# Converting the last pieces of w_in later in the expert loop, and matmuls on a constant ahead of its products

## The chip, the cores and the metric

The kernel runs on one core of a Trainium2 chip. The metric is device microseconds of one execution of the whole program, median of several runs. Engines are named as the profile names them: PE (matmul) with PEld (its weight loads), DVE (VectorE), ACT (ScalarE), POOL (GpSimd) and SP (SyncE, which only issues DMAs here; SPq is its DMA queue). Each engine works through its own list of instructions in order.

## The reference

Three stages follow each other: an attention, a mixture of experts and a two-layer network. Only the middle one is touched by the change, with a piece of the third one's weights.

```python
# moe: x (1792, 768), phi (768, 32), w1 (8, 768, 1024), w2 (8, 1024, 768)
logits = x @ phi
d = softmax(logits, over tokens);  slot_input = d.T @ x        # 32 slots, 4 of each expert
for e in range(8):
    h = maximum(slot_input[e] @ w1[e], 0)
    slot_out[e] = h @ w2[e]
c = softmax(logits, over slots);   x = c @ slot_out
# moe2: w_in (768, 2048) and w_out (2048, 768) as float64, alpha (2048)
h = x @ w_in
g = maximum(h, 0) + alpha * minimum(h, 0)
out = g @ w_out
```

`softmax` stands for the reference's lines of max, exp, sum and division.

## The kernel before, in words

The attention takes the first 300 us or so, in an order that a table of numbers sets. It is the same in both kernels. Then comes the loop over the eight experts (L1325 to L1382), whose order is that of the code, and then the products of the last stage (L1528 to L1530).

**Weights.** w1 and w2 come in 32 units of 128 x 3072 float32 (1536 KB), four of an expert: two halves of w1, two of w2. Below they are numbered 0 to 31. Eleven buffers in five rings hold them; `fetch` (L465) issues the next unit on SP as soon as its buffer is free, which is when PE has used the unit eleven places earlier. From expert 4 on the order on SP is units 23 to 25, then two transfers of w_out, called `rawo` (L1281), then units 26 to 31. The first `rawo` takes the buffer of unit 22 and the second that of unit 23, so they wait for both halves of expert 5's w2 to be used. SP is a queue in order: units 26 to 31 stand behind them.

**One expert.** PE multiplies the slots with w1 (L1339, 24 matmuls in the trace). ACT copies the two halves out of PSUM as `h_sb` (L1350). PE transposes them (L1353, 8). DVE sums each half into `hT` (L1355) and clips it (L1361). PE multiplies hT with w2 (L1370, 16 matmuls for each of two units u).

**Beside it.** `narrow_in(n)` turns piece n of w_in (128 x 768) from the high words of float64 into float32: an Abs on ACT (L540) and five operations on DVE (L541, L543, L545, L548, L551). Pieces 8 to 15 are done here, by the table NARROW two each in experts 0 to 3, after the expert's sums and ahead of its w2 products. Its temporaries share two buffers, so that the Abs of a piece starts when L548 of the piece before it is done. `turn_c(b)`, in experts 2 to 5 for batches 0 to 3, makes the dispatch weights' copies: two casts on DVE (L1262), two subtractions on POOL (L1263), four transposes on PE (L1267), one copy on ACT (L1270, cT). `turn_alpha` in expert 3 turns alpha on PE (L1252) and copies it on DVE (L1253, L1254). `go_early` in expert 6 issues the conversion of the first four blocks of w_out (L498 on ACT, L500 to L510 on DVE, the cast whi L1301 on ACT, the difference wlo L1303 on DVE). Since ACT works in order, h_sb of expert 7 stands behind all of it, and the first wlo overwrites the buffer of unit 27, the second half of expert 6's w2.

Of the kernel before, what the change touches and what calls it, by code (L numbers as in the profile page):

```python
# [12 lines left out]
F16 = mybir.dt.float16  # L13
# [340 lines left out]
def fused_attention_softmoe_mlp(  # L354
# [15 lines left out]
    nc = tc.nc  # L370
    B, H, S, D = q.shape
    NT, DM = out.shape
    E, _, FE = w1.shape
# [3 lines left out]
    P = 128  # L377
# [43 lines left out]
    def pst():  # L421
        return ps.tile([P, 512], F32, tag="t", name="pst", bufs=PST)
# [13 lines left out]
    ident = const.tile([P, P], F32, name="ident")  # L436
# [52 lines left out]
    def prefetch(n):  # L489
        while len(loaded) < min(n, len(items)):  # L490
            for _ in fetch():
                pass
# [43 lines left out]
    def narrow_in(n):  # L536
        g, i = divmod(n, 4)
        w = win[g][:, i * DM : (i + 1) * DM]
        t = hp.tile([P, DM], F32, tag="wf", name="wf", bufs=2)
        nc.scalar.activation(t, w, AF.Abs)  # L540
        nc.vector.tensor_scalar_max(t, t, F64_TINY)  # L541
        b = hp.tile([P, DM], U32, tag="wf", name="wb", bufs=2)
        nc.vector.tensor_copy(b, low[:, (n - N0) * DM : (n - N0 + 1) * DM])  # L543
        t, w = t.bitcast(U32), w.bitcast(U32)
        nc.vector.tensor_scalar(  # L545
            out=t, in0=t, scalar1=3, scalar2=0x3FFFFFFF, op0=ALU.logical_shift_left, op1=ALU.bitwise_and
        )
        nc.vector.scalar_tensor_tensor(  # L548
            out=t, in0=b, scalar=5, in1=t, op0=ALU.logical_shift_right, op1=ALU.bitwise_or
        )  # L550
        nc.vector.scalar_tensor_tensor(  # L551
            out=w, in0=w, scalar=0xC0000000, in1=t, op0=ALU.bitwise_and, op1=ALU.bitwise_or
        )
# [524 lines left out]
    with tc.manual_schedule():  # L1078
# [110 lines left out]
        for o, sp, queue in (("bg0", "bgs", bg), ("pf0", "pfs", pf), ("cv0", "cvs", cv)):  # L1189
            t = T[o]  # L1190
# [30 lines left out]
    for t in range(KD):  # L1221
# [4 lines left out]
            start=True,  # L1226
            stop=True,
# [11 lines left out]
    def psa():  # L1239
        return ps.tile([P, 512], F32, tag="a", name="psa", bufs=6)  # L1240
# [8 lines left out]
    def turn_alpha():  # L1249
        pt = pst()  # L1250
        for t in range(2):
            nc.tensor.transpose(pt[:, t * 8 : t * 8 + 8], alpha_n[:, t::2], ident[: KF // 2, : KF // 2])  # L1252
        nc.vector.tensor_copy(alpha_t, pt[:, :KF].rearrange("p (t n) -> p n t", t=2))  # L1253
        nc.vector.tensor_scalar_mul(nalpha, alpha_t, -1.0)  # L1254
# [3 lines left out]
    def turn_c(b):  # L1258
        c = cN[:, b]
        cs = hp.tile([P, 4, 2, 2, NS], F32, tag="h_sb", name="cs")  # L1260
        for r in range(2):
            nc.vector.tensor_copy(cs[:, :, r, 0, :].bitcast(F32R), c)  # L1262
            nc.gpsimd.tensor_tensor(out=cs[:, :, r, 1, :], in0=c, in1=cs[:, :, r, 0, :], op=ALU.subtract)  # L1263
        pc = pst()
        for j in range(4):
            n = P if j < 3 else D
            nc.tensor.transpose(  # L1267
                pc[:, j * P : j * P + n], cs[:n, j].rearrange("p a b s -> p (a b s)"), ident[:n, :n]
            )
        nc.scalar.copy(  # L1270
            cT4[:, b * S : (b + 1) * S].rearrange("k (p c) -> k c p", c=NC),
            pc[:, :S].rearrange("k (c p) -> k c p", c=NC),
        )
# [5 lines left out]
    def fetch_out(n):  # L1279
        rawo[n] = raw = rings[1 - n % NW // (NW - NWI)][1].tile([P, UNIT], F32, tag="w", name="rawo").bitcast(U32)  # L1280
        nc.sync.dma_start(raw, w_out[2 * n * P : 2 * (n + 1) * P, :].bitcast(U32).rearrange("(p t) f -> p (t f)", p=P))  # L1281
# [33 lines left out]
    def go_early():  # L1315
        for f in EARLY_STEPS:
            next(early[f], None)

    order = ExitStack()
    order.enter_context(tc.manual_schedule())  # L1320
    pS = [psa() for _ in range(2)]
    NARROW = ((8, 9), (10, 11), (12, 13), (14, 15), (), (), (), ())
    for e in range(E):
        n = min(NRING + 4 * e, len(items))
        if len(loaded) <= T["RAWPOS"] < n or (e == E - 1 and not rawo):  # L1325
            prefetch(T["RAWPOS"])
            for i in range(NEARLY // 2):
                fetch_out(i)
        prefetch(n)
        if e == 1:  # L1330
            nc.sync.dma_start(alpha_n, alpha.rearrange("(n f) -> n f", n=KF // 2))
        ph = [psa() for _ in range(2)]
        seen = set()
        todo = [(0, 0, 0), (0, 1, 1), (0, 2, 2), (1, 0, 3), (1, 1, 0), (1, 2, 1)]
        todo += [(0, 3, 3), (0, 4, 0), (0, 5, 1), (1, 3, 2), (1, 4, 3), (1, 5, 0)]
        last = {(hf, g): t for hf, t, g in todo}
        for hf, t, g in todo:
            wu = loaded[0, e, t // 3].rearrange("p (t f) -> p t f", t=3)
            nc.tensor.matmul(  # L1339
                ph[hf][32 * g : 32 * g + 32, :],  # L1340
                slT[:, t, :],
                wu[:, t % 3, hf * 512 : (hf + 1) * 512],
                start=(hf, g) not in seen,
                stop=last[hf, g] == t,
                tile_position=(0, 32 * g),
            )
            seen.add((hf, g))
        for hf in range(2):
            h_sb = hp.tile([P, 512], F32, tag="h_sb", name="h_sb")
            nc.scalar.copy(h_sb, ph[hf])  # L1350
            pt = pst()
            for t in range(4):
                nc.tensor.transpose(pt[:, t * P : (t + 1) * P], h_sb[:, t::4], ident)  # L1353
            dst = hT[:, e, hf * 4 : hf * 4 + 4, SPE * e : SPE * e + SPE]
            nc.vector.tensor_reduce(  # L1355
                out=dst,
                in_=pt.rearrange("p (f g s) -> p f s g", f=4, g=4)[:, :, SPE * e : SPE * e + SPE, :],
                axis=AX.X,
                op=ALU.add,
            )  # L1360
            nc.vector.tensor_scalar_max(dst, dst, 0.0)  # L1361
        if e == E - 2:
            go_early()
        for n in NARROW[e]:
            narrow_in(n)
        for u in range(2):
            wu = loaded[1, e, u].rearrange("p (t f) -> p t f", t=4)
            for hf in range(2):
                for g in range(4):
                    nc.tensor.matmul(  # L1370
                        pS[hf][32 * g : 32 * g + 32, :HD],
                        hT[:, e, 4 * u + g, :],
                        wu[:, g, hf * HD : (hf + 1) * HD],
                        start=(e == 0 and u == 0),
                        stop=(e == E - 1 and u == 1),
                        tile_position=(0, 32 * g),
                    )

        if e == 3:
            turn_alpha()  # L1380
        if 2 <= e < 2 + B:
            turn_c(e - 2)  # L1382

    while len(rings) > 3:
        rings.pop()[0].close()
# [12 lines left out]
    for h in range(2):  # L1398
        pt = pst()
# [233 lines left out]
```

## Time and profile before

| what | us |
|---|---|
| median of 3 runs | 690.39 |
| lowest, highest run | 684.28, 691.68 |
| the profiled execution | 685.3 |
| its span, first to last instruction | 683.3 |

The profile is that of the one execution of 685.3 us. Its times count from the first instruction. A row of the timeline gives start, duration, engine, source line, operation, written and read tile, the shape, how many instructions are merged, and in brackets how long the engine sat idle before it and what released it.

### The profile page before, as it was taken

How to read it: one execution, taken by the hardware profiler on the slowest of the kernel's cores; microseconds unless marked ns; L12 is line 12 of the kernel's file. 1: busy time of each engine (PE TensorE's matmuls, PEld its weight loads, DVE VectorE, ACT ScalarE, POOL GpSimd, SP SyncE). 2: the span in 40 equal slices, each digit the busy share in tenths (PEclk: the TensorE clock that was granted, in tenths of full speed). 3: DMA queues.
4: the chain of work that ended last, by engine and by line, in shares of the span. 5: the costliest groups of instructions: out<-in, count | busy, mean ns of one | idle time of the engine just before them, and what ended most of it. 6: DMA issues, size and time to landing. Idle time of an engine off the chain costs nothing.

```text
span 683.3 us, 14166 instructions
## 1 busy us (share of the span) xinstructions
PE 616.2 (90%) x5670; PEld 475.9 (70%) x5670; DVE 464.9 (68%) x921; ACT 372.4 (54%) x717; POOL 191.6 (28%) x203
## 2 busy tenths in 40 slices
PE   0799998989999999998868668999999999999997
PEld 0367665666667777764323214888899999999997
DVE  5788999998789877735941444999964545454540
ACT  3799998889999998742321223776521111111110
POOL 6976666557657764111001000000000000000000
PEclk9999999999999999999988969999999999999999
DMA  4575677364456325499999799130020101010101
GB/s 138 133 239 165 188 211 204 110 189 126 131 143 200 99 76 171 123 350 391 425 424 395 283 423 400 67 120 0 1 93 1 47 1 47 1 47 0 47 1 46
DMA packets 36240, 106.89 MB, mean 156 GB/s; under 512 B 5448, under 2 KB 22352, under 8 KB 31824
## 3 DMA queue, kind: packets, MB, share of 16 engines
q1 hardware_dynamic: 36176, 106.01, 44.7%
q8 instruction: 44, 0.72, 0.5%
q14 instruction: 20, 0.16, 0.1%
HBM read 92.18 MB, written 5.51 MB: 143 GB/s over the span
## 4 chain that ended last, share of the span: by engine, by line
PE 63%; ACT 14%; DMA 9%; DVE 8%; POOL 4%; issue 2%; SPq 1%; ACTq 0%; POOLq 0%; DVEq 0%
PE psa L1530 12%; PE psa L1529 12%; PE psa L1528 11%; PE psn L818 5%; DMA unit<-in_moe_w_dram 4%; PE psv L878 4%; PE psv L868 3%; PE psa L1339 3%; ACT e L834 3%; PE psr L800 2%; DMA q<-q 2%; ACT psn L839 2%; POOL nf L717 2%; PE psa L1370 2%; ACT sp L723 1%
## 5 line engine op out<-in xcount | busy, mean ns | idle before, releaser
L1528 PE MATMUL psa<-whi,gh 128*128 128x384 f32 (+1 forms) x448 | 152.0, 339 | 0.0
L1529 PE MATMUL psa<-wlo,gh 128*128 128x384 f32 (+1 forms) x448 | 151.1, 337 | 0.0
L1530 PE MATMUL psa<-whi,gl 128*128 128x384 f32 (+1 forms) x448 | 150.8, 337 | 0.0
L809 DVE TENSOR_REDUCE m<-psr 128x1 f16<-128x448 f32 x168 | 97.7, 615 | 4.8 <-PE psr L800 4.6
L1497 ACT CAST gh<-t 128x512 fp32r<-128x512 f32 x40 | 24.9, 621 | 123.0 <-DVE t L1494 122.5
L1529 PEld LDWEIGHTS psa<-wlo,gh 128*128 128x128 f32 x448 | 84.2, 188 | 2.7
L1528 PEld LDWEIGHTS psa<-whi,gh 128*128 128x128 f32 x448 | 84.2, 188 | 2.7
L1530 PEld LDWEIGHTS psa<-whi,gl 128*128 128x128 f32 x448 | 84.1, 188 | 2.8
L878 PE MATMUL psv<-vH,e 128*128 128x65 f16 (+1 forms) x1152 | 84.2, 194 | 0.0
L878 PEld LDWEIGHTS <-e 128*128 128x128 f16 (+1 forms) x1728 | 79.3, 106 | 0.0
L1491 DVE TENSOR_SCALAR t<-pst,alpha_t 128x256 f32<-128x256 f32 x80 | 34.9, 476 | 62.9 <-PE pst L1485 62.9
L868 PEld LDWEIGHTS psv<-vR,e 128*128 128x128 f32 (+1 forms) x384 | 58.9, 176 | 20.0 <-issue 10.8
L878 PE MATMUL psv<-vL,e 128*128 128x64 f16 (+1 forms) x576 | 72.5, 193 | 0.0
L850 POOL TENSOR_TENSOR e<-ef,e 128x448 f16<-128x448 f32 x48 | 52.0, 1083 | 72.2 <-ACT ef L839 52.7
L868 PE MATMUL psv<-vR,e 128*128 128x65 f32 (+1 forms) x384 | 69.8, 263 | 0.2 <-PE psn L818 0.2
L834 ACT ACTIVATE e<-psn 128x448 f16<-128x448 f32 x120 | 65.2, 544 | 7.5 <-PE psn L818 6.2
L818 PE MATMUL psn<-q,k 128*128 128x448 f16 (+1 forms) x192 | 61.4, 361 | 7.3 <-DMA q<-q 2.0
L818 PE MATMUL psn<-qB,kB 67*128 67x448 f16 (+1 forms) x192 | 61.0, 357 | 1.6 <-DMA qB<-mr 1.4
L800 PE MATMUL psr<-k,q 128*128 128x448 f16 (+1 forms) x192 | 57.2, 374 | 3.5 <-ACT k L752 2.8
L850 DVE TENSOR_TENSOR e<-psn,e 128x448 f16<-128x448 f32 x72 | 44.4, 617 | 21.4 <-ACT psn L839 21.2
L730 POOL TENSOR_TENSOR sp<-nf,sp 128x448 f16<-128x448 f32 x48 | 49.8, 1047 | 12.2 <-ACT sp L723 11.8
L745 PE MATMUL pst<-ident,sp 128*128 128x128 f16 x336 | 27.7, 230 | 17.4 <-POOL sp L730 17.4
(178 smaller groups left out, 1091.2 us busy)
## 6 DMA issues: line engine op xcount, KB each, us to landing
unit<-in_moe_w_dram SPq DMA_DIRECT2D x26, 1536.0 KB, 12.2
unit<-in_moe_w_in_dram SPq DMA_DIRECT2D x24, 512.0 KB, 6.8
rawo<-in_moe_w_out_dram SPq DMA_DIRECT2D x8, 1536.0 KB, 13.2
unit<-in_moe_w_dram SPq DMA_DIRECT2D x36, 256.0 KB, 4.9
qk<-in_q_dram SPq DMA_DIRECT2D x12, 448.0 KB, 3.8
qk<-in_k_dram SPq DMA_DIRECT2D x12, 448.0 KB, 5.4
out_dram<-osb SPq DMA_DIRECT2D x14, 384.0 KB, 2.3
vR<-in_v_dram SPq DMA_DIRECT2D x24, 128.0 KB, 3.8
```

Of the source, the lines that this page charges most:

```text
L730: eng.tensor_tensor(out=d["sp"][:, a, :, D:], in0=d["nf"][:, a], in1=d["sp"][:, a, :, 0:D], op=ALU.subtract)
L800: nc.tensor.matmul(pn[o0:o1, :S], d["q"][:, c0 : c0 + o1 - o0], d["k"][:, h * S : (h + 1) * S], start=True, stop=True)
L809: nc.vector.tensor_reduce(out=d["m"][:, c : c + 1], in_=d.pop(("pn", c))[:, :S], axis=AX.X, op=ALU.max)
L818: nc.tensor.matmul(pe[o0:o1, :S], lhs[:, c0 : c0 + o1 - o0], rhs[:, h * S : (h + 1) * S], start=st_, stop=not st_,)
L834: nc.scalar.activation(e2[:, 0], pe[:, :S], AF.Exp, scale=0.125)
L850: eng.tensor_tensor(out=e2[:, 1], in0=ef, in1=e2[:, 0], op=ALU.subtract)
L868: nc.tensor.matmul(pv[o0:o1, slot, :], d["e", c][:, qs], d["vv"][:, h, sl * D : 4 * D + 1], start=(j == 0), stop=False,)
L878: nc.tensor.matmul(pv[o0:o1, slot, 0:wd], d["e", c][:, w // 2, qs], (vl if w == 1 else vh)[:, 4 * h + sl, 0:wd], start=(j == 0 and w == 0) ...
L1491: nc.vector.tensor_scalar(out=t0[:, cs], in0=ph[:, cs], scalar1=0.0, scalar2=alpha_t[:, f // 2, i : i + 1], op0=ALU.min, op1=ALU.mult)
L1528: nc.tensor.matmul(a, gh[f][:, ms], hi[:, hs], start=(f == 0 and not (packed and m % 2 == 1 and hf == 0)), stop=False)
L1529: nc.tensor.matmul(a, gh[f][:, ms], lo[:, hs], start=False, stop=False)
L1530: nc.tensor.matmul(a, gl[f][:, ms], hi[:, hs], start=False, stop=(f == KF - 1 and not (packed and m % 2 == 0 and hf == 1)))
```

## The change

The eight pieces 8 to 15 move from experts 0 to 3 to experts 3 (two), 4 (three) and 5 (three), and within the expert from ahead of its w2 products to the end, behind `turn_alpha` and `turn_c`. A new function `keep_on` writes eight matmuls of 128 x 256 float16 on the identity into a PSUM buffer that is free at that point. It is called from expert 3 on: ahead of each half of the w1 products, and, up to expert 6, ahead of each half of the w2 products. The first PSUM tile of the transposes is allocated at the start of the expert, since keep_on writes there.

```diff
+    def keep_on(e, junk):
+
+        if e >= 3:
+            i16 = ident.bitcast(F16)
+            for _ in range(8):
+                nc.tensor.matmul(junk[:, : 2 * P], i16[:, :P], i16, start=True, stop=True)
+
-    NARROW = ((8, 9), (10, 11), (12, 13), (14, 15), (), (), (), ())
+    NARROW = ((), (), (), (8, 9), (10, 11, 12), (13, 14, 15), (), ())
...
+        pts = [pst(), None]
...
-        for hf, t, g in todo:
+        for i, (hf, t, g) in enumerate(todo):
+            if i % 6 == 0:
+                keep_on(e, pts[0])
...
-            pt = pst()
+            pt = pts[hf] = pts[hf] or pst()
...
-        for n in NARROW[e]:
-            narrow_in(n)
         for u in range(2):
+            if e < E - 1:
+                keep_on(e, ph[0])
...
         if 2 <= e < 2 + B:
             turn_c(e - 2)
+        for n in NARROW[e]:
+            narrow_in(n)
```

On ACT, the list of the experts from the third on stands like this before (h_sb: the expert's two copies; wf<-win: the Abs of w_in's pieces; cT: the dispatch weights; wf<-rawo and whi: go_early):

```order
L1350 COPY h_sb<-psa 128x512 x2
L540 ACTIVATE wf<-win_4271 128x768 x2
L1270 CAST cT_5847<-pst 128x7x64
L1350 COPY h_sb<-psa 128x512 x2
L540 ACTIVATE wf<-win_4271 128x768 x2
L1270 CAST cT_5847<-pst 128x7x64
```

and like this in the changed kernel, for experts 3 to 6:

```order
L1270 CAST cT_5847<-pst 128x7x64
L540 ACTIVATE wf<-win_2854 128x768 x2
L1360 COPY h_sb<-psa 128x512 x2
L1270 CAST cT_5847<-pst 128x7x64
L540 ACTIVATE wf<-win_2854 128x768 x2
L540 ACTIVATE wf<-win_4271 128x768
L1360 COPY h_sb<-psa 128x512 x2
L1270 CAST cT_5847<-pst 128x7x64
L540 ACTIVATE wf<-win_4271 128x768 x3
L1360 COPY h_sb<-psa 128x512 x2
```

The pieces stood ahead of the expert's cT; they now stand behind it, and ahead of the next expert's h_sb.

On DVE, expert 3 before, from its sums to its dispatch casts (the five rows from L541 on are one piece; a second piece stands where the line of dots is):

```order
L1361 TENSOR_SCALAR hT<-hT 128x4x4
L541 TENSOR_SCALAR wf<-wf 128x768
L543 CAST wb<-low 128x768
L545 TENSOR_SCALAR wf<-wf 128x768
L548 SCALAR_TENSOR_TENSOR wf<-wb,wf 128x768
L551 SCALAR_TENSOR_TENSOR win_4271<-win_4271,wf 128x768
...
L1253 COPY alpha_t<-pst 128x16
L1254 TENSOR_SCALAR nalpha<-alpha_t 128x16
L1262 CAST cs<-cN 128x4x32 x2
```

and expert 5 in the changed kernel, from its dispatch casts to expert 6's first sum (two more pieces at the dots):

```order
L1371 TENSOR_SCALAR hT<-hT 128x4x4
L1262 CAST cs<-cN 128x4x32 x2
L541 TENSOR_SCALAR wf<-wf 128x768
L543 CAST wb<-low 128x768
L545 TENSOR_SCALAR wf<-wf 128x768
L548 SCALAR_TENSOR_TENSOR wf<-wb,wf 128x768
L551 SCALAR_TENSOR_TENSOR win_4271<-win_4271,wf 128x768
...
L1365 TENSOR_REDUCE hT<-pst 128x4x4
```

The casts moved ahead of the pieces, and the pieces now stand between one expert's casts and the next expert's sums.

## Rows read from the trace of the kernel before

**Rows 1.** The page's slices: DMA's busy share in tenths, 17.1 us each.

```profile
DMA  4575677364456325499999799130020101010101
```

**Rows 2.** Windows: us, busy time of PE, PEld, DVE, ACT, POOL; clock, DMA, GB/s.

```profile
340.00:350.00 10.00, 5.71 (x26) 1.85 (x27) 3.26 (x7) 0.97 (x1) 0.86 (x2) 0.67 1.00 421
360.00:370.00 10.00, 8.26 (x36) 3.07 (x36) 1.10 (x7) 2.14 (x3) 0.86 (x2) 0.66 1.01 426
...
374.00:375.00 1.00, 1.00 (x16) 0.35 (x11) 0.00 (x0) 0.58 (x1) 0.00 (x0) 1.00 0.54 213
381.00:382.00 1.00, 1.00 (x12) 0.53 (x12) 0.00 (x0) 0.00 (x0) 0.00 (x0) 1.00 1.03 184
```

**Rows 3.** Timeline of SP's queue, issue of the first two rawo.

```profile
380.07 1.62 SPq L1281 DMA_DIRECT2D rawo<-in_moe_w_out_dram  x2
```

**Rows 4.** Waits of SP's queue, 280 to 425 us: total, times, longest.

```profile
SPq L1281 <- PE psa L1370: 15.4, 2, 14.5
```

**Rows 5.** Timeline, expert 3's stall: alpha and dispatch weights behind the pieces.

```profile
355.57 0.40 PE L1252 MATMUL pst<-ident,alpha_n 8*128 8x8 f32 x2
360.09 0.17 DVE L1253 COPY alpha_t<-pst 128x16 f32<-128x16 f32 x1
361.69 1.20 PE L1267 MATMUL pst<-ident,cs 128*128 128x128 f32 x4 [5.72 <-POOL cs L1263]
```

**Rows 6.** Timeline, the end of the experts: go_early, experts 6 and 7.

```profile
387.55 0.56 DVE L500 TENSOR_SCALAR wf<-wf 128x768 f32<-128x768 f32 x1
...
394.07 2.79 PE L1370 MATMUL psa<-unit,hT 128*32 128x384 f32 x16 [7.06 <-DMA unit<-in_moe_w_dram]
...
400.67 0.96 DVE L1303 TENSOR_TENSOR wlo<-wf,whi 128x768 fp32r<-128x768 f32 x1 [6.93 <-PE psa L1370]
...
411.50 1.07 ACT L1350 COPY h_sb<-psa 128x512 f32<-128x512 f32 x2
...
412.13 1.98 PE L1353 MATMUL pst<-ident,h_sb 128*128 128x128 f32 x8 [4.24 <-ACT h_sb L1350]
```

**Rows 7.** Timeline, one expert's steps at the full clock (experts 2, 4, 5).

```profile
335.73 2.79 PE L1370 MATMUL psa<-unit,hT 128*32 128x384 f32 x32
...
370.09 2.79 PE L1370 MATMUL psa<-unit,hT 128*32 128x384 f32 x32
...
372.81 0.75 PE L1267 MATMUL pst<-ident,cs 128*128 128x128 f32 x4
...
373.49 3.62 PE L1339 MATMUL psa<-unit,slT 128*32 128x512 f32 x24
373.59 0.99 ACT L1270 CAST cT<-pst 128x448 fp32r<-128x448 f32 x1 [4.24 <-PE pst L1267]
...
377.04 1.55 PE L1353 MATMUL pst<-ident,h_sb 128*128 128x128 f32 x8
...
378.51 2.79 PE L1370 MATMUL psa<-unit,hT 128*32 128x384 f32 x32
```

**Rows 8.** Timeline, two pieces of w_in in expert 0, then expert 1's sums.

```profile
320.84 0.55 DVE L541 TENSOR_SCALAR wf<-wf 128x768 f32<-128x768 f32 x1
...
323.36 0.85 ACT L540 ACTIVATE wf<-win 128x768 f32<-128x768 f32 x1 [2.96 <-DVE wf L548]
...
324.24 0.56 DVE L541 TENSOR_SCALAR wf<-wf 128x768 f32<-128x768 f32 x1
...
327.64 0.21 DVE L1355 TENSOR_REDUCE hT<-pst 128x16 f32<-128x64 f32 x1
...
328.12 2.79 PE L1370 MATMUL psa<-unit,hT 128*32 128x384 f32 x32
...
328.45 0.55 DVE L541 TENSOR_SCALAR wf<-wf 128x768 f32<-128x768 f32 x1
```

**Rows 9.** Timeline, attention: float16 matmuls of 448 columns, each with a weight load.

```profile
271.16 0.36 PE L818 MATMUL psn<-q,k 128*128 128x448 f16 x1
...
271.35 0.35 PE L818 MATMUL psn<-qB,kB 67*128 67x448 f16 x1
```

## The prediction, made before the changed kernel ran

> **What bounds the kernel now.** I read the slices first, then windows, then SP's queue and the chain through the experts. In the slices DMA is at nine tenths from the end of the attention to the end of the experts, except in one slice of 7 [rows 1]. Windows of 1 us place that dip: traffic halves in the one that begins at 374 and is only just back in the one that begins at 381, so the stream stands still for some 6.5 us [rows 2]. SP's queue says why: the first rawo is issued at 380.07 [rows 3], and its kind waited 14.5 us for the w2 products of expert 5 [rows 4]. Everything behind it on SP, units 26 to 31, waits as well.
>
> PE is late there because it stalled. In expert 3 the turn of alpha is done on PE at 355.97, but DVE copies it only at 360.09, behind two pieces of w_in, and PE sat idle 5.72 us until the dispatch weights were there [rows 5]. The windows of 340 and 360 show the granted clock at a mean of 0.67 and 0.66, where the others next to them are at 1.0: after each of two such stalls PE ran at 1.2 GHz for a while [rows 2].
>
> The loop's end hangs on a second chain. DVE begins go_early at 387.55, does two blocks, and then waits 6.93 us for expert 6's w2 products, which wait for their unit; wlo starts at 400.67, and h_sb of expert 7, behind it on ACT, at 411.50 [rows 6]. What comes later is not changed, so **I forecast the shift of that wlo**.
>
> **The change, part by part.** *Taken away:* the pieces ahead of expert 2's and expert 3's dispatch casts, so two stalls of about 5.7 us and the slow matmuls behind them. Experts 0 to 2 themselves don't start earlier: PE was not held there by more than 0.2 us, so I keep expert 2's w2 products at 335.73 [rows 7].
>
> *Added: keep_on.* One batch is eight matmuls of 256 columns. The nearest row is a float16 matmul of 448 columns with its own weight load, 0.19 us from start to start [rows 9]; 256/448 of it is 0.109, so a batch takes 0.87 us at 2.4 GHz, if loads stay covered as there. Bounds: 0 would need PE to be waiting anyway, which is so for some of the batches; 1.74 if PE is at 1.2 GHz. I take 0.87. A rule of the Trainium skill speaks against the cheap batch: TensorE: Matmul & The Clock Gate, section "LDWEIGHTS (loading the stationary operand)", prices a load at its columns over 1.2 GHz, 107 ns for 128; were it not covered, a batch would be 1.73 us by an estimate from that page and my sum below 5.2 us higher. The row speaks for a covered load.
>
> *Moved: eight pieces.* A piece after another takes 3.40 us on DVE (320.84 to 324.24), two take 6.80 until the next sum, and 0.88 passes from the start of an Abs to DVE's first operation [rows 8]. The pieces now stand behind the expert's cT on ACT and ahead of the next expert's sums on DVE. So each of experts 3 to 5 becomes a ring: w2 products, turn on PE, cT, Abs, the pieces, next sums, next w2 products. I walk it with times of before; S is the start of w2 products.
>
> - Expert 3: from 335.73, 2.72 to the turn (370.09 to 372.81), 0.68 to the w1 products, two batches and 3.55 to the transposes (373.49 to 377.04), 1.55 for these [rows 7], one batch: S3 = 346.84. POOL's part of the dispatch copies is hidden behind the w2 products, as in expert 4.
> - Then 2.72 and a batch to alpha, 0.40 there, 1.60 from DVE's copy of alpha to PE's turn (360.09 to 361.69) [rows 5]: 352.43. Then 0.78 to cT (372.81 to 373.59) and 0.99 for it [rows 7], 0.88 and 6.80 for two pieces: the sums of expert 4 at 361.88. From sums to products 0.48 (327.64 to 328.12) [rows 8]: S4 = 362.36.
> - Expert 4: 2.72 + 0.87 + 0.78 + 0.99 + 0.88 + 3 x 3.40 + 0.48 = 16.92. S5 = 379.28, against 378.51 before [rows 7]. **The long ring gives back all that the stalls were worth.**
> - Expert 5 the same: S6 = 396.20, sums at 395.72.
>
> Transfers don't hold these: unit 23 lands two units ahead of the dip, about 367. The first rawo is issued 0.77 later, and so the dip stays, and unit 27 comes some 0.8 later.
>
> go_early begins 0.81 after expert 6's sums (327.64 to 328.45) [rows 8], at 396.53, 9 us later than before. Its first two blocks take 6.19 of DVE (400.67 less 387.55 less the 6.93 idle) [rows 6]: 402.72. The wait of 6.93 is nearly used up: the products that free the buffer, with unit 27 at about 398.5, are done near 401. So wlo starts at **402.72 instead of 400.67, 2.05 us later**, and h_sb of expert 7, the A stage and all products with it. The batches of experts 6 and 7 lie in DMA waits and cost nothing; if they did not, two of them behind unit 27 would be 1.7.
>
> Against the profiled execution's 685.3 us that is 687.35. It lies 5.1 below the median of 690.39, whose three runs span 684.28 to 691.68; the same 2.05 on the median gives **692.4**. About 1%, 6.9 us, is what a measurement here can tell from no change.
>
> **Rivals.**
>
> *The clock falls in the new gaps: slower.* In expert 5 of the new order w1's products end near 372.0, and h_sb stands on ACT behind the third piece's Abs, done at 375.4; transposes can start at 376.1. PE idles 4.1 us there, and about as long in expert 6; no batch stands in that gap. Before, 4.24 us of idle left the transposes of expert 7 at the lower level, 1.98 against 1.55 us, and sixteen w2 products at that level took 2.79 us [rows 6], as many as 32 at the higher [rows 7]. If expert 5 falls as well, its products and batches lose up to 2.4 (1.39 on the first sixteen and about 1.0 of what follows until the clock is back); if expert 7 stays low through its w2 products, 2.3 more (5.58 against 3.3). With 2.05 that is 6.8, or 697.2, and batches of 1.25 with loads partly uncovered make it 699.4 (six lie on the ring up to S6). It decides once the clock falls in expert 5. Against it: that gap is the shortest of those that I know to have cost the clock. Chance 0.21.
>
> *PE sets expert 5, not DVE: faster.* Without the stalls PE's own path needs 2.72 + 0.87 + 0.68 + 0.87 + 0.87 + 3.55 + 1.55 + 0.87 = 11.98 an expert, and alpha's detour puts S4 at 360.8 and S5 at 372.8. Then the first rawo goes out at 374.4, as the stream runs dry: the dip closes, worth some 6.4, which makes 684.0. The Trainium skill's page on TensorE, section "HAM oscillation", would argue this way: waits between bursts of matmuls cost the clock again each time, and a kernel that stays busy gets that time back. The windows agree that the clock was lost twice [rows 2]. But DVE's list has three pieces between the sums of experts 4 and 5, and 3 x 3.40 can't shrink by 6 us. Chance 0.09.
>
> *The two chains meet: no change.* If cT and Abs overlap and batches are hidden more than I charge, S5 comes at 378 or earlier, wlo waits for unit 27 as before, and the time is 689 to 691. Chance 0.20. That leaves 0.50 for the forecast.
>
> **Range and chances.** The forecast with its bounds runs from 690 to 695. To hold 8 in 10 I add most of the slow rival and part of the fast one, and the spread of runs of one kernel: 684.5 to 698. Faster by over 1% (under 683.5) needs the fast rival whole: 0.07. Slower by over 1% (over 697.3) needs the clock and dear batches together: 0.14. Within 1%: 0.79.
>
> **What would show it.** Right: in the changed trace no stall ahead of the turns of experts 3 and 4; clock at 1.0 from 340 to 370; pieces 10 to 12 back to back right ahead of expert 5's sums at about 379; the first rawo near 381 with the dip still there; DVE's idle ahead of the first wlo under 2 us, and wlo near 403. Wrong: expert 5's w2 products before 375 or after 383, a batch over 1.2 us, the stream without a dip, or a shift in the attention.

## The result: slower, and by more than forecast

| what | before | changed kernel |
|---|---|---|
| median, us | 688.75 (20 runs) | 693.43 (20 runs) |
| lowest, highest run | 684.28, 695.38 | 689.96, 699.18 |
| ratio of the runs, 95% interval | | 1.008 [1.0058, 1.0103] |
| the profiled execution, its span | 685.3, 683.3 | 689.96, 687.9 |
| mean granted clock of PE | 0.975 | 0.981 |

The forecast was 692.4, 2.0 above the median then known (690.39). Over twenty runs that median is 688.75, the medians differ by 4.7, and the ratio makes it 5.5. The ratio's interval is clear of 1, though the difference is under the 1% that the prediction set for telling a change. Ratios leave out the executions in a slower state that a few runs show, and they are not quotients of the medians.

The slices of the page of the changed kernel answer to [rows 1]: a slice of 7 among the nines there, slices of 8 and 6 here.

```profile
DMA  4576676464457326499998699140020101010101
```

Windows of the changed kernel, to be held against [rows 2] (us, busy time of PE, PEld, DVE, ACT and POOL with their instructions in brackets, granted clock, DMA share, GB/s):

```profile
340.00:350.00 10.00, 9.94 (x78) 4.76 (x77) 0.80 (x4) 2.14 (x3) 0.00 (x0) 1.00 1.01 424
350.00:360.00 10.00, 8.38 (x57) 3.79 (x55) 3.93 (x9) 2.45 (x3) 0.87 (x2) 0.83 1.01 423
360.00:370.00 10.00, 9.94 (x84) 4.98 (x82) 4.31 (x12) 2.04 (x4) 0.88 (x2) 1.00 1.01 424
...
376.00:378.00 2.00, 0.00 (x0) 0.00 (x0) 1.97 (x3) 1.31 (x3) 0.00 (x0) 1.00 0.15 61
...
380.00:382.00 2.00, 1.75 (x10) 0.72 (x12) 1.90 (x8) 0.00 (x0) 0.00 (x0) 0.50 0.00 0
...
384.00:386.00 2.00, 2.00 (x23) 0.78 (x20) 0.00 (x0) 0.00 (x0) 0.00 (x0) 1.00 0.74 209
```

The stalls go, as forecast: from 340 to 350 PE is busy 9.94 us of 10 where it was busy 5.71, at the full clock where it had 0.67. Then PE stops from 376 to 378 while DVE is busy throughout, and the stream runs dry at the place where it ran dry before. The first rawo, in SP's queue, comes at 383.44, after a wait of 16.3 us for expert 5's w2 products; [rows 3] had 380.07 and [rows 4] 14.5 us:

```profile
383.44 2.72 SPq L1281 DMA_DIRECT2D rawo<-in_moe_w_out_dram  x2
```

The waits of SP's queue in the changed kernel, whole span (total, times, longest):

```profile
SPq L1281 <- PE psa L1380: 18.3, 2, 16.3
```

The timeline of the changed kernel, in three pieces. First experts 3 and 4, answering to [rows 5] and [rows 7] (start, duration, engine, line, operation, tiles, shape, count, and idle time before it with its releaser):

```profile
348.34 1.50 PE L1380 MATMUL psa<-unit,hT 128*32 128x384 f32 x16
...
354.19 0.75 PE L1267 MATMUL pst<-ident,cs 128*128 128x128 f32 x4 [1.62 <-POOL cs L1263]
354.87 1.75 PE L1324 MATMUL pst<-ident 128*128 128x256 f16 x8
356.56 2.83 PE L1349 MATMUL psa<-unit,slT 128*32 128x512 f32 x12
...
363.54 1.04 PE L1324 MATMUL psa<-ident 128*128 128x256 f16 x8
364.50 1.50 PE L1380 MATMUL psa<-unit,hT 128*32 128x384 f32 x16
365.94 1.05 PE L1324 MATMUL psa<-ident 128*128 128x256 f16 x8
366.91 1.50 PE L1380 MATMUL psa<-unit,hT 128*32 128x384 f32 x16
368.34 0.75 PE L1267 MATMUL pst<-ident,cs 128*128 128x128 f32 x4
```

The stall of 5.72 us in expert 3 is gone; what is left of alpha's detour is an idle 1.62. Expert 4's turn at 368.34 has no idle time in front. Then the ring of expert 5, with ACT and DVE:

```profile
369.13 0.97 ACT L1270 CAST cT<-pst 128x448 fp32r<-128x448 f32 x1 [6.23 <-PE pst L1267]
369.89 0.85 ACT L540 ACTIVATE wf<-win 128x768 f32<-128x768 f32 x1
370.77 0.56 DVE L541 TENSOR_SCALAR wf<-wf 128x768 f32<-128x768 f32 x1 [6.32 <-ACT wf L540]
...
376.69 0.84 ACT L540 ACTIVATE wf<-win 128x768 f32<-128x768 f32 x1 [2.56 <-DVE wf L548]
...
377.44 1.05 ACT L1360 COPY h_sb<-psa 128x512 f32<-128x512 f32 x2
...
378.06 1.43 PE L1363 MATMUL pst<-ident,h_sb 128*128 128x128 f32 x8 [3.33 <-ACT h_sb L1360]
...
379.29 1.91 PE L1324 MATMUL psa<-ident 128*128 128x256 f16 x8
...
380.97 0.22 DVE L1365 TENSOR_REDUCE hT<-pst 128x16 f32<-128x64 f32 x1
...
381.45 1.92 PE L1380 MATMUL psa<-unit,hT 128*32 128x384 f32 x16 [0.25 <-DVE hT L1371]
```

Between the turn and the next sums DVE does 10.20 us of pieces (370.77 to 380.97), one behind the other. PE is done with expert 5's w1 products, but h_sb stands on ACT behind the third Abs, and the sum stands on DVE behind the third piece. At last the loop's end, which answers to [rows 6]:

```profile
399.01 0.55 DVE L500 TENSOR_SCALAR wf<-wf 128x768 f32<-128x768 f32 x1
...
405.11 0.95 DVE L1303 TENSOR_TENSOR wlo<-wf,whi 128x768 fp32r<-128x768 f32 x1
...
415.91 1.07 ACT L1360 COPY h_sb<-psa 128x512 f32<-128x512 f32 x2
```

DVE's wait of 6.93 us ahead of the first wlo is gone entirely, and yet wlo is later: go_early began at 399.01 where it began at 387.55 (10.1 us later, counted from the copy of the slots described next).

**How the time splits.** The attention ends with the copy of the slots (slT, DVE L1229), and the loop with the first copy of `s_sb`. The stretch behind it takes 266.5 to 266.8 us in every trace taken. In the table all places are us behind the start of slT; "residue" is a kernel's median less its loop, or less the mean of its two loops. The medians come from different chips; before's own median moved between 687.22 and 688.75 from one set of runs to another.

| run | slT at | expert 5's sums | first rawo | first wlo | loop | median | residue |
|---|---|---|---|---|---|---|---|
| before | 315.00 | 62.82 | 65.07 | 85.67 | 101.79 | 688.75 | 586.1 |
| before_again | 318.34 | 63.16 | 65.41 | 86.01 | 103.58 | | |
| changed | 316.33 | 64.64 | 67.11 | 88.78 | 105.03 | 693.43 | 588.3 |
| after_again | 321.10 | 64.65 | 66.69 | 88.37 | 105.29 | | |
| e1_keep_alone | 317.22 | 70.17 | 73.30 | 92.81 | 109.04 | 698.01 | 589.0 |
| e2_move_alone | 319.67 | 60.24 | 63.57 | 84.16 | 101.43 | 689.76 | 588.3 |
| e3_place_alone | 318.75 | 60.20 | 62.45 | 83.28 | 99.72 | 686.90 | 587.2 |
| e4_place_keep | 316.55 | 61.55 | 64.68 | 84.09 | 100.32 | 685.33 | 585.0 |
| e5_keep_double | 316.54 | 71.61 | 73.65 | 96.21 | 113.71 | 700.65 | 586.9 |
| e6_no_13_15 | 319.55 | 64.64 | 67.20 | 86.12 | 101.64 | 690.42 | 588.8 |
| e7_spread | 317.56 | 51.11 | 53.53 | 80.77 | 97.20 | 683.33 | 586.1 |
| e8_spread_keep6 | 316.96 | 51.43 | 54.14 | 80.79 | 97.22 | 682.35 | 585.1 |
| e10_spread_split | 314.83 | 50.47 | 52.92 | 78.88 | 93.59 | 680.66 | 587.1 |

The loop is 2.5 us longer for the change (mean of two traces each, and before's two differ by 1.8), and its first wlo is 2.7 later, against 2.05 forecast. The other 2 us of the medians are not found in the loops traced. Ahead of the loop and behind it both kernels hold the same instructions.

### The profile page after: what moved, and what is told of

It is laid out like the page before. It is cut to its first block, busy times and chain, and to the rows that moved or that the text cites. A ratio compares the mean times of both kernels' runs of the same rounds, so it can differ in the third digit from the quotient of the medians.

```text
span 687.9 us, 14455 instructions
## 1 busy us (share of the span) xinstructions
PE 629.8 (92%) x5814; PEld 489.4 (71%) x5814; DVE 465.1 (68%) x921; ACT 372.0 (54%) x717; POOL 192.2 (28%) x203
## 4 chain that ended last, share of the span: by engine, by line
PE 65%; ACT 16%; DVE 6%; DMA 6%; POOL 4%; issue 3%; SPq 0%; ACTq 0%; POOLq 0%; DVEq 0%
PE psa L1542 11%; PE psa L1541 11%; PE psa L1540 11%; PE psn L818 4%; DMA unit<-in_moe_w_dram 4%; PE psv L878 4%; PE psv L868 3%; ACT e L834 3%; PE psa L1380 3%; PE psa L1349 3%; PE psr L800 2%; ACT psn L839 2%; POOL nf L717 2%; ACT sp L723 2%; PE pst L1497 1%
```

## The experiments

The theory: the batches and the pieces' new place are two changes of opposite sign, and the ring of three pieces sets the time. The rivals: the batches are free and the clock they hold is a gain; the clock lost in the new gaps is what makes it slower; the place behind the copies is no gain at all. Each diff is against the changed kernel, and "before" is that of the same chips.

**e1_keep_alone**: the batches alone, pieces where they were.

```diff
-    NARROW = ((), (), (), (8, 9), (10, 11, 12), (13, 14, 15), (), ())
+    NARROW = ((8, 9), (10, 11), (12, 13), (14, 15), (), (), (), ())
...
+        for n in NARROW[e]:
+            narrow_in(n)
         for u in range(2):
...
-        for n in NARROW[e]:
-            narrow_in(n)
```

> The batches of the change alone; the pieces of w_in stay where they were, in experts 0 to 3. Theory 1 (the ring of w2 products, turn, cT, Abs, pieces and sums sets experts 4 to 6, and a batch costs about 1 us wherever PE is on the path): the stalls ahead of the turns of experts 2 and 3 stay, so the batches of expert 3 start at the low clock (1.75 us each) and lie on PE's path up to expert 5; its w2 products come some 10 us later than before, the first rawo too, and the time is 8 to 12 us above before (697 to 701). Rival (what counts is the clock, and batches keep it up): the clock comes back sooner and the time falls by 2 to 4 us.

Measured: 698.01 against 687.22, ratio 1.0169 [1.0139, 1.0200]. The batches alone are no gain: the median is 10.8 us above before, as expected. In the trace expert 5's sums come 7.2 later (I had some 10) and the loop is 6.4 longer than the mean of before's two; the rest of the 10.8 is not in this loop. Its timeline, the turns behind experts 2 and 3, each with the batch that follows:

```profile
346.50 1.20 PE L1267 MATMUL pst<-ident,cs 128*128 128x128 f32 x4 [5.76 <-POOL cs L1263]
347.63 1.89 PE L1324 MATMUL pst<-ident 128*128 128x256 f16 x8
...
366.18 0.81 PE L1267 MATMUL pst<-ident,cs 128*128 128x128 f32 x4 [3.74 <-POOL cs L1263]
366.92 1.89 PE L1324 MATMUL pst<-ident 128*128 128x256 f16 x8
```

The first stall is as long as before (5.76, and 5.77 in the trace of before); the second, that of [rows 5], shrinks from 5.72 to 3.74. The clock falls behind both, and the batch there takes 1.89 us at the lower level. Batches that stand behind a stall don't prevent it; they are more work for the slow stretch.

**e2_move_alone**: the pieces moved as in the change, no batches.

```diff
-            if i % 6 == 0:
-                keep_on(e, pts[0])
...
-            if e < E - 1:
-                keep_on(e, ph[0])
```

> The pieces' move alone, without any batch. Theory 1: the ring is shorter by six batches, w2 products of expert 5 at about 375 instead of 380 (counted as in the trace of before), first rawo near 377, the dip of the DMA stream down to about 3 us, the first wlo near 398: 1 to 3 us below before, some 6 below the change. Rival: without batches PE's clock falls in experts 4 and 5 and the time is no better than the change's, 4 to 8 us above before.

Measured: 689.76 against 687.22, ratio 1.0042 [1.0020, 1.0064]: below the changed kernel, by 3.7 by the medians and 2.6 by the ratios, but not below before. I had the sign wrong. In its trace the first wlo comes 1.7 earlier than in before (mean of two; I had 2.7), and the loop of 101.43 is a little under before's 101.79 and 103.58, so what raises the median is not in this loop, and no run here shows where it lies. What the move gains in the loop is small, since the gaps that it leaves cost the clock:

```profile
377.00 1.98 PE L1361 MATMUL pst<-ident,h_sb 128*128 128x128 f32 x8 [5.44 <-ACT h_sb L1358]
...
380.39 4.08 PE L1376 MATMUL psa<-unit,hT 128*32 128x384 f32 x32 [1.41 <-DVE hT L1369]
```

The 32 w2 products take 4.08 us where [rows 7] has 2.79. So the move by itself is no gain here, and what the change adds to it in the loop is the batches': 105.16 less 101.43, 3.7 us.

**e3_place_alone** and **e4_place_keep**: the new place behind the copies, but the old table, two pieces in each of experts 0 to 3; without and with the batches.

```diff
-    NARROW = ((), (), (), (8, 9), (10, 11, 12), (13, 14, 15), (), ())
+    NARROW = ((8, 9), (10, 11), (12, 13), (14, 15), (), (), (), ())
```

(e3_place_alone also leaves out the four lines of e2_move_alone.)

> Only the place within the expert: pieces behind the dispatch weights' copies, but in experts 0 to 3, two each, as before; no batches. Theory 1: the rings of experts 2 and 3 have two pieces each, experts 4 to 6 are free of them and run at PE's own 8.4 us; w2 products of expert 5 at about 371.5, first rawo at 373, ahead of the end of the stream, so the dip closes: 5 to 6.5 us below before. Rival (the expert loop's end is not tied to the dip): within 2 us of before.

> As the run with the place alone, with the change's batches. Theory 1: from expert 3 on PE needs 12.4 us an expert instead of 8.4, so w2 products of expert 5 come at about 376, the first rawo near 378, the dip is 4 us long: about 2 us below before and some 4 above the run without batches. Rival (batches keep the clock and are worth it): as fast as or faster than the run without.

Measured against 687.22: e3 686.90, ratio 0.9993 [0.9971, 1.0014], and e4 685.33, ratio 0.9967 [0.9942, 0.9992]. e4 came out as expected against before, e3 did not: I had it 5 to 6.5 below, and e4 some 4 above it, where e4 is as fast or faster, as its rival said. The timeline of e3_place_alone, experts 3 and 4:

```profile
349.95 1.24 PE L1361 MATMUL pst<-ident,h_sb 128*128 128x128 f32 x8 [2.05 <-ACT h_sb L1358]
353.33 4.16 PE L1376 MATMUL psa<-unit,hT 128*32 128x384 f32 x32 [2.15 <-DVE hT L1369]
...
366.13 1.24 PE L1361 MATMUL pst<-ident,h_sb 128*128 128x128 f32 x8 [0.81 <-ACT h_sb L1358]
...
369.52 4.48 PE L1376 MATMUL psa<-unit,hT 128*32 128x384 f32 x32 [2.15 <-DVE hT L1369]
```

and its window from 350 to 360 (columns as above):

```profile
350.00:360.00 10.00, 6.24 (x45) 2.96 (x45) 4.09 (x13) 0.38 (x1) 0.86 (x2) 0.81 1.02 428
```

Two idles of 2.05 and 2.15 us with 1.24 us of transposes between them were enough: the products behind take 4.16. In the next expert the idles are 0.81 and 2.15, and the products take 4.48. In e4 a batch fills the second idle but for 0.96 us, and the clock stays, as e4_place_keep's timeline of the same products shows:

```profile
351.10 1.50 PE L1380 MATMUL psa<-unit,hT 128*32 128x384 f32 x16 [0.96 <-DVE hT L1371]
```

Yet the two loops are 99.72 and 100.32. An expert with nothing to wait for takes 8.43 us in e3 (sums of expert 5 to those of 6) and 12.52 in e4: 4.1 us for four batches. What the batches save in clock they cost in time, as far as one trace of each tells.

**e5_keep_double**: a batch has sixteen matmuls.

```diff
-            for _ in range(8):
+            for _ in range(16):
```

> The change with sixteen matmuls in each batch in place of eight. Theory 1 (a batch costs what it takes, wherever it lies between w2 products, turn and sums on the ring): about six more batches of 1 us on the way to expert 6's sums, so the first wlo comes 6 us later and the time is 5 to 8 us above the change (699 to 702). Rival (batches lie in waits, and the more there is the better the clock holds): within 1.5 us of the change, or below it.

Measured: 700.65 against 688.15, ratio 1.0185 [1.0142, 1.0228], 7.2 above the changed kernel, as expected. Its loop is 8.6 longer (113.71 against 105.16), so the batches are on the path. The timeline of e5_keep_double, one doubled batch:

```profile
390.06 1.92 PE L1324 MATMUL psa<-ident 128*128 128x256 f16 x16
```

Its row is 1.92 us long where that of a single batch is 1.05 (365.94 in the changed kernel): the eight matmuls added take 0.87 us, 0.109 each.

**e6_no_13_15**: pieces 13 to 15 of w_in are not converted, so expert 5 has none.

```diff
-    NARROW = ((), (), (), (8, 9), (10, 11, 12), (13, 14, 15), (), ())
+    NARROW = ((), (), (), (8, 9), (10, 11, 12), (), (), ())
```

> The change with expert 5's three pieces left out (pieces 13 to 15 of w_in stay unconverted). Theory 1 (the chain through the pieces sets the first wlo, not the DMA stream): expert 6's sums come some 5 us earlier, after which the wait for expert 6's w2 products and its unit is next, at about 1.5 to 3 us behind before: 1.5 to 3 us below the change, no more. Rival (the pieces of expert 5 are the whole loss): back to before or below, 4.7 us or more under the change.

Measured: 690.42 against 688.15, ratio 1.0039 [1.0010, 1.0067], 3.0 below the changed kernel, at the edge of what I expected. Expert 6's sums come 5.4 us earlier, the first wlo only 2.7, since now it waits again, as the timeline shows:

```profile
405.67 0.96 DVE L1303 TENSOR_TENSOR wlo<-wf,whi 128x768 fp32r<-128x768 f32 x1 [2.21 <-PE psa L1380]
```

So the last ring is on the path, and 2.7 us below it lies the other chain, that of unit 27.

**e7_spread**: the new place, the pieces spread so that no ring is long, no batches.

```diff
-    NARROW = ((), (), (), (8, 9), (10, 11, 12), (13, 14, 15), (), ())
+    NARROW = ((8, 9), (10, 11), (12,), (13,), (14,), (15,), (), ())
...
-            if i % 6 == 0:
-                keep_on(e, pts[0])
...
-            if e < E - 1:
-                keep_on(e, ph[0])
```

> The pieces spread: two each in experts 0 and 1, one each in experts 2 to 5, all behind the copies, and no batches. Theory 1: a ring with one piece is 9.3 us against PE's own 8.4, so PE idles under 1 us at a time and keeps the clock; w2 products of expert 5 at about 365 to 367 in the times of before, the first rawo ahead of the end of the stream, no dip: 5 to 6.5 us below before. Rival (the dip is not what the end hangs on): within 2 us of before.

Measured: 683.33 against 688.15, ratio 0.9953 [0.9920, 0.9987]: 4.8 by the medians, 3.2 by the ratio, a little under what I expected. Its windows where the dip was:

```profile
370.00:380.00 10.00, 5.12 (x48) 1.50 (x39) 2.85 (x5) 1.60 (x2) 0.78 (x2) 1.00 1.01 424
380.00:390.00 10.00, 3.34 (x20) 1.51 (x20) 5.98 (x12) 2.85 (x4) 0.00 (x0) 0.83 1.01 425
```

and its timeline, expert 3's w2 products and the first wlo:

```profile
349.04 2.79 PE L1376 MATMUL psa<-unit,hT 128*32 128x384 f32 x32 [0.55 <-DVE hT L1369]
...
398.33 0.96 DVE L1303 TENSOR_TENSOR wlo<-wf,whi 128x768 fp32r<-128x768 f32 x1 [6.93 <-PE psa L1376]
```

With one piece in an expert PE idles 0.55 us ahead of the w2 products, keeps the clock without a single filler, and is done with expert 5 before the stream needs its buffers. The dip is gone: 424 and 425 GB/s where [rows 2] halves. The dip came from units that waited for expert 5, and here they don't. e2 differs from e7 by the table alone, and its ratio is 1.0042 where e7 has 0.9953: that is the gain that the change's own table, with its pieces packed late, gave away.

**e8_spread_keep6**: e7 with batches in experts 6 and 7 alone (`if e >= 3` becomes `if e >= 6`, with the change's calls and e7's table).

> As the run with the pieces spread, with the batches in experts 6 and 7 alone. There PE waits for DMA and loses the clock; the second half of expert 6's w2 products, on which the first wlo waits, took 2.79 us at the low clock. Theory: they come at the high clock, 1 to 1.5 us below the spread run, 6 to 8 below before. Rival: batches in a wait change nothing, equal to the spread run.

Measured: 682.35 against 688.15, ratio 0.9922 [0.9890, 0.9954], not told apart from e7, and the loops are equal: 97.20 and 97.22. So the rival holds, as far as these runs tell. The timeline of e7_spread, the second half of expert 6's w2 products:

```profile
395.43 2.79 PE L1376 MATMUL psa<-unit,hT 128*32 128x384 f32 x16 [0.92 <-DMA unit<-in_moe_w_dram]
```

and that of e8_spread_keep6, both halves:

```profile
391.73 2.79 PE L1380 MATMUL psa<-unit,hT 128*32 128x384 f32 x16 [6.91 <-DMA unit<-in_moe_w_dram]
...
396.13 1.50 PE L1380 MATMUL psa<-unit,hT 128*32 128x384 f32 x16
```

The batch between the halves brings the second half to 1.50 us but makes it wait: counted from slT it begins at 79.17 instead of 77.87 and ends at 80.67 instead of 80.66, and the wlo behind it comes at the same place. One batch ahead of a wait of 7 us doesn't hold the clock through it.

**e10_spread_split**: e7, with go_early cut in two: the conversion of its last block and its last two wlo follow expert 7's sums instead of standing ahead of expert 7's h_sb. The first wlo, which waits for unit 27, stays ahead of it.

```diff
+    EARLY_TAIL = [2, 3, 3, 3, 3, 3, 2, 3, 3]
+    EARLY_HEAD = [0, 1, 0, 0, 0, 0, 0, 2, 1, 1, 1, 1, 0, 1, 2, 2, 2, 2, 1]
+
-    def go_early():
-        for f in EARLY_STEPS:
+    def go_early(steps):
+        for f in steps:
...
-        if e == E - 2:
-            go_early()
+        if e >= E - 2:
+            go_early(EARLY_HEAD if e == E - 2 else EARLY_TAIL)
```

> The spread run with go_early cut: its last block of w_out is converted behind the sums of expert 7 instead of ahead of its h_sb. Theory 1 (h_sb of expert 7 stands behind the last cast on ACT, and this hands on every delay of the first wlo): PE's last w2 products follow unit 31, about 3 us earlier than in the spread run, some 8 below before (about 680). Rival (unit 31 sets the end anyway, or the block's conversion returns in the copies behind the loop): within 1 us of the spread run.

Measured: 680.66 against 688.42, ratio 0.9919 [0.9876, 0.9963]. The loop is 3.6 shorter than e7's, where I had about 3, and this version beats both kernels. Its timeline at the end of the loop:

```profile
392.10 1.50 PE L1379 MATMUL psa<-unit,hT 128*32 128x384 f32 x16 [0.92 <-DMA unit<-in_moe_w_dram]
...
393.71 0.96 DVE L1303 TENSOR_TENSOR wlo<-wf,whi 128x768 fp32r<-128x768 f32 x1 [5.65 <-PE psa L1379]
...
400.51 0.58 ACT L1361 COPY h_sb<-psa 128x512 f32<-128x512 f32 x1 [4.20 <-PE psa L1350]
...
406.89 1.50 PE L1379 MATMUL psa<-unit,hT 128*32 128x384 f32 x16 [2.21 <-DMA unit<-in_moe_w_dram]
...
408.42 0.55 DVE L1407 COPY s_sb<-psa 128x384 f32<-128x384 f32 x1
```

The last products wait for their unit, and nothing of go_early holds them up any more: the loop now ends on the stream. But not all of the 3.6 is the cut's. The first wlo, which stands ahead of the cut, already comes 1.9 earlier than in e7 (78.88 against 80.77): the w2 products in front of it began 0.6 earlier and ran at the full clock, 1.50 us instead of 2.79. From the first wlo to the end of the loop it is 14.7 us here, 16.4 in e7 and 15.5 to 17.6 in the other traces; that leaves about 1.7 for the cut. The intervals of e7, e8 and e10 overlap.

**before_again** and **after_again**: another look at either kernel, unchanged, on one chip.

> The kernel before once more, for a second trace. If attention and tail only scatter, the loop from the slot copy to the copy of its result takes 101.8 us again within 1 us (100.8 to 102.8), and the slot copy lies anywhere between 315 and 320. If the scatter is in the loop, it differs by more.

> The changed kernel once more, for a second trace. Theory 1: the loop takes 105.0 us within 1 us again, 3.2 more than before; the rest of the 4.7 us between the medians is scatter of the attention. Rival: the loop itself is typically 4 to 5 us longer than before's, and the first trace was a lucky one.

Measured: 690.39 and 694.78, spans 688.5 and 693.0. For before I had a loop within 1 us of 101.8; it is 103.58, a miss. The changed kernel's, 105.29, lies where I had it, but 1.7 above that of before_again and not 3.2. The timeline of before_again where the attention ends:

```profile
318.34 0.36 DVE L1229 COPY slT<-pst 128x192 f32<-128x192 f32 x1 [1.57 <-PE pst L1222]
```

and that of after_again there and in expert 5:

```profile
321.10 0.36 DVE L1229 COPY slT<-pst 128x192 f32<-128x192 f32 x1 [1.81 <-PE pst L1222]
...
382.85 1.24 PE L1363 MATMUL pst<-ident,h_sb 128*128 128x128 f32 x8 [3.34 <-ACT h_sb L1360]
...
386.23 1.50 PE L1380 MATMUL psa<-unit,hT 128*32 128x384 f32 x16 [1.27 <-DVE hT L1371]
```

The table's places in the loop repeat to 0.4 us up to the first wlo; what lies behind it repeats to 1.5 us, and the copy of the slots to 4.8. And in expert 5's gap the clock held this time: 1.50 us for the products that took 1.92 in the first trace.

## Why the prediction was right in kind and short in size

By its own steps, each counted from slT (315.00 in the profile of before):

- **The stalls go, and nothing starts earlier in expert 2.** Right: S3 was forecast at 31.84 and came at 32.01.
- **A batch costs 0.87 us.** Mis-sized: 0.97 from the first matmul to the product behind the batch (365.94 to 366.91). The eight matmuls are not what was wrong: at the full clock they start 0.109 us apart, which e5's doubled batch confirms. It is the step that was left out, from the last of them to the next product, which takes 0.20 us and not 0.11. Six batches on the ring up to S6 make 0.6. Loads stay covered: the 144 loads of the batches take 98 ns each (median; 147 at the lower level) beside the matmuls. The Trainium skill, TensorE: Matmul & The Clock Gate, section "Back-to-back issue gap", gives 109 ns from one matmul of 256 columns to the next as the figure of a lone matmul without a load; the trace agrees with the figure, and has it with a load for every matmul. By the price that the Trainium skill's section "LDWEIGHTS (loading the stationary operand)" on the same page gives a load, uncovered loads would have made a batch 1.73 us, an estimate; the trace does not bear it out.
- **S4 at 47.36.** 48.17. The sums came 0.21 late; the rest is PE. Its clock fell after alpha's detour (354.87: a batch of 1.75, then 2.83 for the w1 products that take 1.91), so that the w2 products began 1.08 after the sums and not 0.48. I had charged that detour as time, not as clock, and the sign "clock at 1.0 from 340 to 370" failed in its middle window (0.83).
- **The ring of three pieces takes 16.92.** Right in sum: 381.45 less 364.50 is 16.95. There is some luck in it: PE needs 3.84 to the turn and not 3.59, and the Abs starts 0.76 behind the start of cT and not 0.99.
- **Expert 6's sums at 80.72.** 82.00 and 81.59. In the first of these traces the clock fell in expert 5's gap (0.50 from 380 to 382; the products took 1.92 instead of 1.50), in the second it did not, and expert 6's sums come 0.4 earlier for it.
- **go_early begins behind them, and its blocks take 6.19; wlo 2.05 later.** The step holds: 6.78 and 6.78 from sums to wlo against 7.00 forecast. wlo is 2.7 later (mean of two traces each), the loop 2.5.
- **The dip stays, rawo later.** Right, 1.3 to 2.0 later instead of 0.8.

So the chain and its direction are shown: e6 shortens the ring and the time falls, e5 lengthens the batches and it rises, and e7 takes both away, and the stalls and the dip are gone together. The 0.5 to 0.7 us by which the loop and its first wlo exceed the forecast are, as far as the steps tell, the batch's price and the clock after alpha.

That the median of 693.43 lies only 1.0 from the 692.4 forecast is luck in part: the median of before was taken 1.6 too high from three runs, and the shift 2.6 too low.

**The rivals.** That the clock falls in the new gap of expert 5 was right about one trace of two, for 0.4 us and not the 2.4 I had given it: the gap was 3.33 us where I had 4.1, and the clock was back by the second half of the products. Expert 7's products, to which I had given 2.3 more, took 3.48 and 4.14 us, and 3.31 and 4.75 in the two traces of before: a scatter, no loss of the change. That PE sets expert 5 and closes the dip did not happen here. It did in e7. That e7's 683.33 is near the 684.0 of that rival says little, since the base differs: the gain is 4.8 by the medians and 3.2 by the ratio, and the rival had 6.4. What stood against it, three pieces in a row on DVE, was the right reason. The Trainium skill's section "HAM oscillation" on the same page says that waits between bursts cost the clock each time, and advises an order of the loop in which PE stays warm. e3's and e2's rows agree with the first half, and e7, which shortens the waits by order, with the second. It is matmuls put in for the clock alone that don't pay: in e4 they cost what they save. That the two chains meet was near: e6 shows unit 27's chain 2.7 us below.

**What stays open.** The medians differ by 4.7, the loops by 2.5. The copy of the slots lies between 314.83 and 321.10 in 13 traces, in which PE, DVE and ACT do the same attention instructions in the same order, 316.7 and 318.7 on average for the two traces of before and of the change, and the residues of the table scatter from 585.0 to 589.0 over kernels that share the attention and the tail. The missing 2 us are of that size, and so are the differences of median that e1 and e2 leave outside the loop. Whether the changed program is truly later in the attention these runs don't settle: two profiles of a kernel are too few against a scatter of 6 us. I had listed a shift in the attention as a sign of being wrong; with one trace of each it can't be read at all.

## What to carry to other kernels

Work that is moved off one wait lands on the next in-order queue: follow the whole ring (here products, turn, copy, Abs, pieces, sums, products) and keep each turn of it under the bound engine's own time, by spreading the pieces one to a turn rather than by packing them late. Matmuls put in to hold the clock are paid for in full wherever PE is on the path, and do nothing behind a stall that they stand after; shortening the gaps held the clock for nothing here. When an edit removes a stall, look for the next queue entry that holds others up (here the last block of go_early, in front of h_sb): cutting go_early there was worth about 1.7 us of loop, once the rings were short.

## What the runs showed of the hardware that I had not expected

- One gap of the same length, in the same kernel, kept the clock once and lost it once: 3.33 us of idle ahead of transposes, then sixteen products in 1.92 us (granted clock 0.50 from 380 to 382), and 3.34 us of idle, then 1.50 us. Two shorter idles, 2.05 and 2.15 us with 1.24 us of transposes between, lost it too.
- Float16 matmuls of 256 columns, each with its own weight load of 98 ns, start 0.109 us apart at the full clock and 0.213 apart at the lower level (347.63 in e1): the load lies covered. The product behind a batch, which is of another kind, starts 0.20 us after the batch's last matmul.
- Identical instructions of the attention end 6.3 us apart from one execution to the next (314.83 to 321.10), while the expert loop behind them repeats to under 2 us.
